# A fused adaLN, scan and SwiGLU kernel: the FFN's products in pairs of 64 rows instead of single products of 128

## The chip, the cores and the metric

The kernel runs on one core of a Trainium2 chip. Times are device microseconds of that core; the time of a kernel is the median of its runs. Lower is better.

## The reference

`x` is 2048 tokens (rows) by D = 448 channels, F = 1792, one state-space layer with N = 256 states a channel, all in float32.

```python
mod = (silu(c) @ w_mod).reshape(1, 6, 1, 448)         # sa, ca, ga, sb, cb, gb
h = layernorm(x) * (1 + ca) + sa
x = x + ga * S4(h)                                    # causal convolution over the 2048 rows + h * Dskip
h = layernorm(x) * (1 + cb) + sb
x = x + gb * ((silu(h @ w_gate) * (h @ w_up)) @ w_down)
```

Float32 accuracy is kept by splitting each operand of the large products into a high part in float32r and a remainder (`hi`, `lo`); three products are summed: hi times hi, hi times the weight's lo, lo times the weight's hi.

## The kernel before

The 2048 rows are 16 tiles of 128 rows. A preamble computes the modulation, the short form of the convolution (a cumulative sum over rows, a product with a triangular matrix `tri`, taken when a flag read at run time allows it; the profile is of that path) and the first two tiles. Then eight blocks of two tiles (256 rows) follow. In each, the FFN runs over NF = 14 chunks of 128 columns of F, called steps here, and the scan and the norms of the next block's two tiles are done beside it.

A step f, in the function `ffn`:

- `gate_up` (products at L758): h is kept transposed as `hhi`, `hlo`, four chunks of 128 channels by 256 rows. 448 channels are three and a half chunks; the last chunk holds the same 64 channels twice, once to meet the weight's hi, once its lo, so that hi times hi and hi times lo are seven products, lo times hi four: 11 for gate, then 11 for up, each of 256 columns into one bank of PSUM (`bank`, a pool of four).
- the gating: SILU on ACT (L773), its product with up on DVE (L788), `phi` on ACT (L795), `plo` on DVE (L796). The last step of a block does this in two halves (L781 to L784).
- `down` (L808) of the step before: per tile three products of 448 columns, summed over the 14 steps in the banks `dn` (DN[0] and DN[1]). It stands behind the gate/up of step f, so `down(f - 1)` is asked for a whole step after its inputs' gate/up has ended. After the last step the sums are scaled by `gb` and added to x (L865, L866), and x is stored.
- in block 0 the weights come from memory and are split into hi and lo (`split_w` at L122 to L125, two steps ahead, and `split_d` at L115 to L117); later blocks find them split.

The scan's stages of a tile are `s0` (norm, two operations on DVE), `s1` (two products), `rows` and `s2` (add the carried row `run`, split into vh and vl), `s3`, `s4` (three products with `tri`, L978 to L980, into the bank CV and a pool bank) and `s5` (carry row, sums added to x). Then `n2.stat`, `n2.root` (POOL), `make_xn` (DVE, the root applied by ACT) and `turn` (a transpose by DVE and five transfers through memory). `split_turned` writes the next block's `hhi` and `hlo`, with the shift `sbc` added.

Nothing schedules this at run time: the order of a queue is the order in which the program is written. `TIMES` gives for each stage the half step (two to a step) behind which it is written: `todo[(f, 0)]` ahead of the down products, `todo[(f, 1)]` behind.

## Time and profile before

| | |
|---|---|
| time, median of 3 runs (range) | 466.75 us (466.59 to 467.31) |
| span of the profiled execution | 465.0 us |
| lying around the span, taken against the median | 1.7 us |
| PE busy | 455.2 us, 98% |
| weight loads (PEld) busy | 434.4 us, 93% |
| DVE busy | 294.4 us, 63% |
| ACT busy | 171.7 us, 37% |
| first gate/up product of block 0 | 32.6 us into the span |

The profile is of one execution. PE is the matmul itself, PEld its weight load, which runs beside the matmul before. In a timeline row the first number is the start, the second how long the row's group lasted; a trailing bracket is the engine's idle time before it and what ended it. [...]

### The profile page before, as it was taken

To read this page: it belongs to the slowest core of one execution; us is meant where nothing else is said; L and a number is where in the kernel's file an instruction comes from. 1 tells how busy PE (TensorE), PEld (TensorE's weight loads), DVE (VectorE), ACT (ScalarE), POOL (GpSimd) and SP (SyncE) were. 2 spreads that over 40 slices of the span, in tenths; PEclk is the share of its full clock that TensorE was granted. 3 is DMA by queue.
4 is the path that set the end of the run, shared out by engine and by line. 5 is a ranking of instruction groups with operands and counts; after the bars stand their busy time and mean duration, and the time that the engine had idled before them with its cause. 6 is when DMAs were issued, how large, how long until landed. Compare 5 with 4: busy or idle time off the path is not lost.

```text
span 465.0 us, 8496 instructions
## 1 busy us (share of the span) xinstructions
PE 455.2 (98%) x3339; PEld 434.4 (93%) x3339; DVE 294.4 (63%) x614; ACT 171.7 (37%) x433; POOL 74.3 (16%) x99
## 2 busy tenths in 40 slices
PE   7899999999999999999999999999999999999996
PEld 4469999999999999999999999999999999999995
DVE  4888999868736676457746766467745775353224
ACT  4889656522333233322323233322333223332121
POOL 2142001000110521023210431005210331000000
PEclk9999999999999999999999999999999999999999
DMA  8975553010112001120022001120012101110001
GB/s 301 406 266 176 196 196 107 24 57 2 47 45 81 1 0 48 47 79 2 28 65 80 1 0 47 47 80 0 24 56 58 37 2 45 47 61 23 1 1 45
DMA packets 20947, 32.92 MB, mean 71 GB/s; under 512 B 2849, under 2 KB 15265, under 8 KB 20897
## 3 DMA queue, kind: packets, MB, share of 16 engines
q1 hardware_dynamic: 20256, 32.10, 20.0%
q8 instruction: 28, 0.46, 0.4%
q10 hardware_dynamic: 640, 0.18, 0.2%
q14 instruction: 23, 0.18, 0.1%
HBM read 25.40 MB, written 6.82 MB: 69 GB/s over the span
## 4 chain that ended last, share of the span: by engine, by line
PE 95%; issue 2%; DMA 1%; DVE 1%; POOL 0%; ACT 0%; POOLq 0%; ACTq 0%
PE bank L758 61%; PE dn L808 28%; DMA vec<-in_c_log_dt_dram 1%; PE dn L480 1%; PE cv L978 1%; PE bank L979 1%; PE cv L980 1%; PE bank L266 0%; PE bank L403 0%; POOL rsa L186 0%; PE cv L991 0%; PE bank L437 0%; ACT L339 0%; PE bank L836 0%; PE cv L375 0%
## 5 line engine op out<-in xcount | busy, mean ns | idle before, releaser
L758 PE MATMUL bank<-hhi,gu 128*128 128x256 f32 x1568 | 216.4, 278 | 0.1
L758 PEld LDWEIGHTS bank<-hhi,gu 128*128 128x128 f32 x1568 | 203.7, 188 | 3.7 <-issue 0.8
L758 PE MATMUL bank<-hlo,gu 128*128 128x256 f32 x896 | 138.6, 277 | 0.0
L758 PEld LDWEIGHTS bank<-hlo,gu 128*128 128x128 f32 x896 | 118.5, 188 | 0.2
L788 DVE TENSOR_TENSOR bank<-raw,bank 128x256 f32<-128x256 f32 x91 | 38.7, 426 | 82.1 <-PE bank L758 69.3
L795 ACT CAST phi<-bank 128x256 fp32r<-128x256 f32 x104 | 38.7, 372 | 132.4 <-DVE bank L788 132.4
L773 ACT ACTIVATE raw<-bank 128x256 f32<-128x256 f32 x98 | 37.5, 383 | 90.5 <-PE bank L758 86.9
L796 DVE TENSOR_TENSOR plo<-bank,phi 128x256 fp32r<-128x256 f32 x104 | 44.1, 424 | 40.8 <-ACT phi L795 40.8
L808 PE MATMUL dn<-wdh,phi 128*128 128x448 f32 x220 | 62.3, 364 | 0.0
L808 PE MATMUL dn<-wdh,plo 128*128 128x448 f32 x220 | 62.2, 363 | 0.0
L808 PE MATMUL dn<-wdl,phi 128*128 128x448 f32 x220 | 61.7, 362 | 0.0
L808 PEld LDWEIGHTS dn<-wdh,plo 128*128 128x128 f32 x220 | 41.2, 188 | 2.9 <-DVE plo L796 0.3
L808 PEld LDWEIGHTS dn<-wdl,phi 128*128 128x128 f32 x220 | 41.2, 187 | 2.6
L808 PEld LDWEIGHTS dn<-wdh,phi 128*128 128x128 f32 x220 | 34.8, 188 | 0.8 <-ACT p L773 0.2
L185 POOL TENSOR_SCALAR rsb<-mvb 128x1 f32<-128x1 f32 (+1 forms) x15 | 8.8, 584 | 115.0 <-DVE mvb L157 115.0
L185 POOL TENSOR_SCALAR rsa<-mva 128x2 f32<-128x2 f32 x8 | 1.9, 243 | 134.2 <-DVE mva L157 131.9
L215 ACT ACTIVATE raw<-raw,rsb 128x64 f32<-128x64 f32 x14 | 4.9, 349 | 34.6 <-POOL rsb L186 33.6
L125 DVE TENSOR_TENSOR gu<-raw,gu 128x1024 fp32r<-128x1024 f32 x14 | 17.1, 1219 | 0.9 <-ACT gu L123 0.9
L953 POOL TENSOR_TENSOR m<-m,gm 128x448 f32<-128x448 f32 x10 | 11.5, 1154 | 25.2 <-DVE m L202 25.2
L959 DVE TENSOR_TENSOR v<-v,run 1x448 fp32r<-1x448 f32 x14 | 13.3, 949 | 0.0
L967 DVE TENSOR_TENSOR vl<-m,vh 128x448 fp32r<-128x448 f32 x12 | 7.4, 617 | 8.9 <-ACT vh L966 8.8
L972 POOL TENSOR_TENSOR m<-m,gd 128x448 f32<-128x448 f32 x10 | 12.9, 1292 | 0.4
(240 smaller groups left out, 425.5 us busy)
## 6 DMA issues: line engine op xcount, KB each, us to landing
raw<-in_B_w_gate_up_dram SPq DMA_DIRECT2D x14, 512.0 KB, 3.3
rawd<-in_B_w_down_dram SPq DMA_DIRECT2D x16, 224.0 KB, 3.5
xd<-raw SPq DMA_DIRECT2D x12, 256.0 KB, 2.0
raw<-xd SPq DMA_DIRECT2D x48, 64.0 KB, 1.9
x<-in_A_u_dram SPq DMA_DIRECT2D x12, 224.0 KB, 2.9
out_dram<-x SPq DMA_DIRECT2D x11, 224.0 KB, 2.0
wm<-in_w_mod_groups_dram SPq DMA_DIRECT2D x5, 448.0 KB, 8.3
wm<-in_w_mod_groups_dram SPq DMA_DIRECT2D x5, 336.0 KB, 8.2
```

Of the source, the lines that this page charges most:

```text
L125: ve.tensor_tensor(wgu[j][:, :, 3:7, :], w[:, :, ::-1, :], f32(wgu[j][:, :, 0:4, :][:, :, ::-1, :]), op=OP.subtract)
L185: po.tensor_scalar(rs[:, 0:n], self.mv[:, 0:n, 1], EPS, None, op0=OP.add)
L758: pe.matmul(ps[s][:, 0:n], w[:, s, a], (hlo if lo else hhi)[:, k, first_col(n):first_col(n) + n], start=first and q == 0, stop=end and q = ...
L773: sc.activation(p[:, 0:n], ps[0][:, 0:n], AF.Silu)
L788: ve.tensor_tensor(ps[1][:, 0:n], p[:, 0:n], ps[1][:, 0:n], op=OP.mult)
L795: sc.copy(hi[:, 0:n], ps[1][:, 0:n])
L796: ve.tensor_tensor(lo[:, 0:n], ps[1][:, 0:n], f32(hi[:, 0:n]), op=OP.subtract)
L808: pe.matmul(dn[q][:, 0:D], u[:, cs], v, start=f == 0 and z == 0, stop=f == (NF - 3 if last else NF - 1) and z == 2)
L953: (ve if on_v else po).tensor_tensor(v, h, g, op=OP.mult)
L959: ve.tensor_tensor(v1[0:1], f32(v1[0:1]), run1[0:1], op=OP.add)
L967: ve.tensor_tensor(vl, v0, f32(vh), op=OP.subtract)
L972: (ve if on_v else po).tensor_tensor(h, h, gd, op=OP.mult)
```

## The change

The transposed h and the gate and up weights are laid out in seven chunks of 64 channels. Partitions 0 to 63 of a weight chunk hold gate, 64 to 127 hold up; h stands twice, in both halves. A product uses 64 rows of the array, and products are issued in pairs, one on the upper and one on the lower 64 rows (`both`): gate above into one bank, up below into another, 21 pairs a step (7 chunks times three parts). The weight load of a step is 448 KB instead of 512 KB.

The down sums are pairs too. Of a chunk of 128 columns of F the upper half holds 64, the lower half the other 64. In step f (`point`) the upper rows work for one tile and the lower rows for the other (`first`, of step f - 1); what is left, the other halves, follows at the next step's point (`rest`, of step f - 2), with the halves' tiles exchanged. So at a point each bank is written by one half alone. A point stands behind `POINT[f]` gate/up pairs: 18, and 14 in a block's first and last step. A block's last sums therefore fall into steps 0 and 1 of the next block, and there `leave` scales and stores them; blocks take the banks DN[0], DN[1] and DN[2], CV in turn (`SUMS`). The scan's three products with `tri` become six halves over two points, in the other block's banks.

Besides: the norm's root and shift are applied on DVE in `make_xn`; `split_turned` has no shift to add, and writes 1792 columns of hlo where 1024 were; `ident` lives in the preamble alone, block 0 turns its next tiles through memory as the others do; `TIMES` has ten entries a tile.

```diff
+POINT = [14] + [18] * 12 + [14]
-    ((2, 3), 3, ((4, 5, 7, 8, 10, 11, 12), (7, 8, 13, 14, 16, 17, 18))),
+    ((2, 3), 3, ((4, 5, 7, 8, 10, 12, 13, 13, 14, 16), (7, 8, 14, 15, 16, 18, 18, 18, 19, 20))),
...
+    SUMS = [DN[0:2], [DN[2], CV]]
...
     def make_xn(i, to):
...
+        ve.scalar_tensor_tensor(to, xs[i], m, cbw, op0=OP.subtract, op1=OP.mult)
+        ve.scalar_tensor_tensor(to, to, rs, sb, op0=OP.mult, op1=OP.add)
...
+    def split_turned(part):
+        for ks in (LOW, HIGH):
+            for q in range(2):
+                src = turned[q].rearrange("p a k r -> p k a r")[:, ks]
+                hi, lo = (h[:, ks, cols(q)].rearrange("p k (a r) -> p k a r", a=4) for h in (hhi, hlo))
+                if part == 0:
+                    sc.copy(hi, src)
+                else:
+                    ve.tensor_tensor(lo, src, f32(hi), op=OP.subtract)
...
+        def both(top, low):
+            done = []
+            for pair in zip_longest(top, low):
+                for e, op in zip(halves, pair):
+                    if op:
+                        o, w, r, start, stop = op
+                        done.append(pe.matmul(o, w[e], r[e], start=start, stop=stop).ins)
+            return done
...
+            def gate_up(f):
+                w, ps = wgu[f], [bank(), bank()]
+                prod = [(0, hhi), (1, hhi), (0, hlo)]
+                if fresh and f < 2:
+                    order = [(z, k) for z in range(3) for k in range(7)]
                 else:
+                    order = [(z, k) for k in range(7) for z in range(2)] + [(2, k) for k in range(7)]
+                ops = [(w[:, prod[z][0], k], prod[z][1][:, k], q == 0, q == 20) for q, (z, k) in enumerate(order)]
+                return ps, [[(t[:, 0:n], *o) for t in ps] for o in ops]
...
+            def first(f):
+                def half(c, begin, end):
+                    return [[(*down(f, q, z), begin and z == 0, end and z == 2) for z in range(3)] for q in (c, 1 - c)]
+                rest.append((half(1 - f % 2, False, f == (NF - 3 if last else NF - 1)), leave if f == NF - 1 else None))
+                return half(f % 2, f == 0, False)
+            def leave():
+                for q, i in enumerate(ts):
+                    ve.tensor_tensor(sums[q][:, 0:D], sums[q][:, 0:D], gb, op=OP.mult)
+                    ve.tensor_tensor(xs[i], xs[i], sums[q][:, 0:D], op=OP.add)
+                    sy.dma_start(out[i * 128:(i + 1) * 128, :], xs[i])
...
+            def point(f):
+                take = first if f else ahead.pop() if ahead else None
+                left = [rest.pop()] if rest else []
+                ops = [[], []]
+                if take and not (last and f == NF - 1):
+                    ops = take((f - 1) % NF)
+                for g, i in todo.get((f, "pe"), []) + todo.get((f - 1, "pe2"), []):
+                    ops = [u + v for u, v in zip(ops, g(i))]
...
+                for more, _ in left:
+                    ops = [u + v for u, v in zip(ops, more)]
+                done = both(*ops)
...
             for f in range(NF):
...
+                ps, ops = gate_up(f)
+                ops = list(zip(*ops))
+                both(ops[0][:POINT[f]], ops[1][:POINT[f]])
+                point(f)
+                both(ops[0][POINT[f]:], ops[1][POINT[f]:])
+                if f == NF - 1 and not last:
+                    split_turned(0)
+                gating(f, ps, f + 2 if fresh and f + 2 < NF else None)
+                if f == NF - 1 and not last:
+                    split_turned(1)
...
+        def first_half(i):
+            h, vh, vl, v1 = vs[i]
+            o, r = sums_for(i)
+            return [(o, tri, vh, True, False), (o, tri, vl, False, False)], [(r, tri, v1, True, False)]
+        def second_half(i):
+            h, vh, vl, v1 = vs[i]
+            o, r = sums_for(i)
+            return [(r, tri, v1, False, True)], [(o, tri, vh, False, False), (o, tri, vl, False, True)]
```

In the new kernel every product of the FFN has one line (L753, in `both`), the gating keeps L788, L795 and L796, SILU is L774, `leave` is L818 and L819, `make_xn` L209 and L210, the split weights L124 and L126, the hlo of the next block L255.

PE, one step of a steady block, before: 22 gate/up products (gate's 11, then up's 11), then the six down products of the step before.

```order
L758 MATMUL bank<-hhi,gu_609 128x256 x7
L758 MATMUL bank<-hlo,gu_609 128x256 x4
L758 MATMUL bank<-hhi,gu_609 128x256 x7
L758 MATMUL bank<-hlo,gu_609 128x256 x4
L808 MATMUL dn_68<-wdh_664,phi 128x448
L808 MATMUL dn_69<-wdh_664,phi 128x448
L808 MATMUL dn_68<-wdl_665,phi 128x448
L808 MATMUL dn_69<-wdl_665,phi 128x448
L808 MATMUL dn_68<-wdh_664,plo 128x448
L808 MATMUL dn_69<-wdh_664,plo 128x448
```

PE, a step after: 36 halves (18 pairs), then at the point the newest step's three pairs and, of the step before that, the other halves (four of their six products are shown; six more gate/up halves follow).

```order
L753 MATMUL bank<-hhi,gu_984 128x256 x28
L753 MATMUL bank<-hlo,gu_984 128x256 x8
L753 MATMUL dn_68<-wdh_1062,phi 128x448
L753 MATMUL dn_69<-wdh_1062,phi 128x448
L753 MATMUL dn_68<-wdl_1063,phi 128x448
L753 MATMUL dn_69<-wdl_1063,phi 128x448
L753 MATMUL dn_68<-wdh_1062,plo 128x448
L753 MATMUL dn_69<-wdh_1062,plo 128x448
L753 MATMUL dn_68<-wdh_986,phi 128x448
L753 MATMUL dn_69<-wdh_986,phi 128x448
L753 MATMUL dn_68<-wdl_987,phi 128x448
L753 MATMUL dn_69<-wdl_987,phi 128x448
```

The down products of the newest step moved from behind the next step's 22 gate/up products to behind 18 of its 21 pairs, and half of each step's sums moved one step later.

DVE, the boundary of two steady blocks, before: the last step's gating in halves, the next block's hlo, the four operations that scale the sums and add them to x, then the gating of step 0.

```order
L781 TENSOR_TENSOR raw<-raw,bank 128x128 x2
L784 TENSOR_TENSOR plo<-raw,phi 128x128 x2
L220 SCALAR_TENSOR_TENSOR hlo<-raw,sbc,hhi 128x256 x4
L865 TENSOR_TENSOR dn_68<-dn_68,gb 128x448
L866 TENSOR_TENSOR x_74<-x_74,dn_68 128x448
L865 TENSOR_TENSOR dn_69<-dn_69,gb 128x448
L866 TENSOR_TENSOR x_75<-x_75,dn_69 128x448
L788 TENSOR_TENSOR bank<-raw,bank 128x256
```

DVE, the same place after:

```order
L781 TENSOR_TENSOR raw<-raw,bank 128x128 x2
L784 TENSOR_TENSOR plo<-raw,phi 128x128 x2
L255 TENSOR_TENSOR hlo<-raw,hhi 128x4x128 x2
L255 TENSOR_TENSOR hlo<-raw,hhi 128x3x128 x2
L788 TENSOR_TENSOR bank<-raw,bank 128x256
L796 TENSOR_TENSOR plo<-bank,phi 128x256
L818 TENSOR_TENSOR dn_70<-dn_70,gb 128x448
L819 TENSOR_TENSOR x_74<-x_74,dn_70 128x448
L818 TENSOR_TENSOR cv<-cv,gb 128x448
L819 TENSOR_TENSOR x_75<-x_75,cv 128x448
L788 TENSOR_TENSOR bank<-raw,bank 128x256
```

The four operations moved behind the gating of step 0 and stand ahead of that of step 1; they read sums that PE ends in step 1.

DVE, a steady block, steps 8 to 10 before: `s5` of the second tile (L1000 to L1003), a gating, its statistics and the one operation of `make_xn` (L212), the next gating.

```order
L981 TENSOR_TENSOR x_73<-m_79,x_73 128x448
L1000 SCALAR_TENSOR_TENSOR run<-run,cv 32x448
L1002 TENSOR_TENSOR x_73<-x_73,cv 128x448
L1003 SCALAR_TENSOR_TENSOR x_73<-bank,tok,x_73 128x448
L788 TENSOR_TENSOR bank<-raw,bank 128x256
L796 TENSOR_TENSOR plo<-bank,phi 128x256
L156 BN_STATS stb<-x_73 128x6
L157 BN_AGGR mvb<-stb 128x2
L212 SCALAR_TENSOR_TENSOR raw<-x_73,mvb,cbw 128x448
L788 TENSOR_TENSOR bank<-raw,bank 128x256
```

DVE, the same work after, between the gatings of steps 9 and 10:

```order
L796 TENSOR_TENSOR plo<-bank,phi 128x256
L1032 SCALAR_TENSOR_TENSOR run<-run,dn_70 32x448
L1034 TENSOR_TENSOR x_73<-x_73,dn_70 128x448
L1035 SCALAR_TENSOR_TENSOR x_73<-cv,tok,x_73 128x448
L157 BN_STATS stb<-x_73 128x6
L158 BN_AGGR mvb<-stb 128x2
L209 SCALAR_TENSOR_TENSOR raw<-x_73,mvb,cbw 128x448
L210 SCALAR_TENSOR_TENSOR raw<-raw,rsb,sb 128x448
L788 TENSOR_TENSOR bank<-raw,bank 128x256
```

All seven operations now stand in one gap between two gatings, and L210 reads `rsb`, the root that POOL computes from L158's result.

## The prediction

> **What bounds the kernel now.** I read the page's busy times, then the chain that ended last, then the timeline of one step.

> ```profile
> span 465.0 us, 8496 instructions
> PE 455.2 (98%) x3339; PEld 434.4 (93%) x3339; DVE 294.4 (63%) x614; ACT 171.7 (37%) x433; POOL 74.3 (16%) x99
> PE bank L758 61%; PE dn L808 28%; DMA vec<-in_c_log_dt_dram 1%; PE dn L480 1%; PE cv L978 1%; PE bank L979 1%; PE cv L980 1%; PE bank L266 0%; PE bank L403 0%; POOL rsa L186 0%; PE cv L991 0%; PE bank L437 0%; ACT L339 0%; PE bank L836 0%; PE cv L375 0%
> ```

> PE is busy almost throughout, and its gate/up products (L758) and down products (L808) are 89% of the chain. A step f of the FFN, in order of time:

> ```profile
> 203.17 0.96 PE L758 MATMUL bank<-hhi,gu 128*128 128x256 f32 x7
> 204.42 0.56 PE L808 MATMUL dn<-wdh,phi 128*128 128x448 f32 x2
> 206.88 0.96 PE L758 MATMUL bank<-hhi,gu 128*128 128x256 f32 x7
> ```

> The 11 products of the up half run from 203.17 to 204.42, 0.1136 us each. One step is 206.88 - 203.17 = 3.71 us: 22 such products (2.50) and six of 448 columns (1.21, 0.2017 each). So a column costs 0.44 to 0.45 ns in both, and the stream has no gap. There are 8 x 14 = 112 steps. The span lies 1.7 us under the median of the runs (466.75); I sum against 465.0 and add that back.

> **The change: the products.** Gate/up goes from 22 products to 21 pairs, down from 6 to 6 pairs. What a pair of 64-row products costs, no row shows. Ends: 0.1136, since each half still streams its 256 columns, so I exclude less; and 0.227, two in turn. The nearest rows are the preamble's products in column tiles, beside whole-array products of the same length (25.34 to 26.09: two passes, 0.375 each):

> ```profile
> 17.20 0.57 PE L266 MATMUL bank<-wm,cs 128*32 128x448 f32 x3
> 17.60 0.55 PE L266 MATMUL bank<-wm,cs 128*32 128x448 f32 x3
> 25.34 0.92 PE L480 MATMUL dn<-v,tri 128*128 128x448 f32 x2
> 26.09 0.92 PE L480 MATMUL dn<-hd,ident 128*128 128x448 f32 x2
> 17.20 0.12 PEld L266 LDWEIGHTS bank<-wm,cs 128*32 128x32 f32 x3 [0.17 <-issue]
> L266 PEld LDWEIGHTS bank<-wm,cs 128*32 128x32 f32 x24 | 0.7, 107 | 0.7 <-issue 0.4 <-DMA wm<-in_w_mod_groups_dram 0.2
> L758 PEld LDWEIGHTS bank<-hhi,gu 128*128 128x128 f32 x1568 | 203.7, 188 | 3.7 <-issue 0.8
> ```

> Three tiles' passes take 0.40 us, what one alone takes, and three loads of 107 ns are over in 0.12. Tiles of the array work side by side, so I take 0.1136 and 0.2017 a pair: **-0.1136 x 112 = -12.7 us**, and a step of 21 x 0.1136 + 6 x 0.2017 = 3.60.

> A load grows by (188 - 107)/96 = 0.84 ns a column, so 128 columns hold the load path 108 of every 114 ns. [...]

> Scan products: three of 448 columns a tile before, now six halves in two points, where each point has eight on one half and seven on the other: four pair times instead of three, 14 tiles x 0.20 = **+2.8**. The end of block 0 loses its PE transposes and two tiles their two-pass products: **-1** (estimate from their few 0.1 us each).

> **The change: what PE now waits for.** Before, gate ended half a step before up, so SILU (L773) lay beside up. Now gate and up end together. Let T be the time at which a step's last gate/up product has been streamed. The rows of the chain, once with SILU as the last to come, once with SILU after its products (the next products start at 241.49):

> ```profile
> 236.38 0.36 ACT L773 ACTIVATE raw<-bank 128x256 f32<-128x256 f32 x1
> 236.77 0.43 DVE L788 TENSOR_TENSOR bank<-raw,bank 128x256 f32<-128x256 f32 x1 [2.12 <-ACT raw L773]
> 237.24 0.37 ACT L795 CAST phi<-bank 128x256 fp32r<-128x256 f32 x1 [0.50 <-DVE bank L788]
> 237.64 0.42 DVE L796 TENSOR_TENSOR plo<-bank,phi 128x256 fp32r<-128x256 f32 x1 [0.44 <-ACT phi L795]
> 241.49 0.96 PE L758 MATMUL bank<-hhi,gu 128*128 128x256 f32 x7
> 241.75 0.38 ACT L773 ACTIVATE raw<-bank 128x256 f32<-128x256 f32 x1 [1.61 <-PE bank L758]
> 82.39 0.42 DVE L796 TENSOR_TENSOR plo<-bank,phi 128x256 fp32r<-128x256 f32 x1
> 82.86 0.30 PEld L808 LDWEIGHTS dn<-wdh,plo 128*128 128x128 f32 x2 [0.28 <-DVE plo L796]
> ```

> SILU starts 0.26 after T, the product L788 at T+0.65, phi ends at T+1.49, plo at T+1.94; PE takes it 0.05 later. The new order asks for phi after 18 pairs (T+2.05) and for plo two down pairs on (T+2.45). Cushion: 2.45 - 1.99 = 0.46 us. Before, the down products came a whole step after T, and a late L788 did no harm:

> ```profile
> 223.58 0.56 PE L808 MATMUL dn<-wdh,phi 128*128 128x448 f32 x2
> 225.97 0.42 DVE L788 TENSOR_TENSOR bank<-raw,bank 128x256 f32<-128x256 f32 x1
> 227.90 0.56 PE L808 MATMUL dn<-wdh,phi 128*128 128x448 f32 x2
> ```

> Here L788 ran 2.39 after T, and PE did not wait. Now DVE is free at T+1.94 and the next L788 is due at T+3.60+0.65 = T+4.25: 2.30 us of other DVE work fit, 0.46 more goes into the cushion, and beyond 2.76 PE waits. By the new order, a block of the steady kind:

> ```profile
> 196.49 0.62 DVE L865 TENSOR_TENSOR dn<-dn,gb 128x448 f32<-128x448 f32 x1
> 198.89 0.42 DVE L788 TENSOR_TENSOR bank<-raw,bank 128x256 f32<-128x256 f32 x1
> 193.58 0.48 DVE L781 TENSOR_TENSOR raw<-raw,bank 128x128 f32<-128x128 f32 x2 [2.43 <-PE bank L758]
> 103.41 0.60 DVE L958 TENSOR_TENSOR m<-m,run 1x448 f32<-1x448 f32 x1
> 105.19 0.68 DVE L200 SCALAR_TENSOR_TENSOR m<-rawd,mva,ca 128x448 f32<-128x448 f32 x1
> 106.51 0.42 DVE L788 TENSOR_TENSOR bank<-raw,bank 128x256 f32<-128x256 f32 x1
> 65.25 0.63 DVE L1000 SCALAR_TENSOR_TENSOR run<-run,cv 32x448 f32<-32x448 f32 x1
> 67.16 0.61 DVE L117 TENSOR_TENSOR wdl<-rawd,wdh 128x448 fp32r<-128x448 f32 x1
> 233.10 0.62 DVE L156 BATCH_NORM_STATS2 stb<-x 128x6 f32<-128x448 f32 x1
> 233.75 0.18 DVE L157 BATCH_NORM_AGGREGATE mvb<-stb 128x2 f32<-128x6 f32 x1
> 234.82 0.57 POOL L186 TENSOR_TENSOR rsb<-rsb,halves 128x1 f32<-128x1 f32 x1
> 53.23 0.83 ACT L122 CAST gu<-raw 128x768 fp32r<-128x768 f32 x1
> 59.09 1.22 DVE L125 TENSOR_TENSOR gu<-raw,gu 128x1024 fp32r<-128x1024 f32 x1
> 60.22 0.42 DVE L796 TENSOR_TENSOR plo<-bank,phi 128x256 fp32r<-128x256 f32 x1
> ```

> - **leave** (four operations, 196.49 to 198.89, 2.40 us) now stands between the sums of step 1 and its L788. Those sums end three pairs (0.34) before T; add 0.26 for the lag: DVE is through at T+2.32, L788 is 1.67 late, PE waits 1.67 - 0.46 = 1.21.
> - **hlo of the next block**: from L781 (193.58) to the end of the old hlo work (196.49) are 2.91; it had 1024 columns in four, now 1792, at L125's rate (1.13/1024) 0.38 longer. So the low four chunks are there at about T+3.2 and the rest at T+4.07; PE asks at T+2.80, and four pairs later. Waits 0.42 and 0.40.
> - **Steps 4 and 8**: rows, vl, and two s0 operations take 3.10 (103.41 to 106.51): 0.34 over. At step 8 the same amount follows a step 7 that ends 0.46 late; less 0.40 for the longer point: 0.40.
> - **Step 10**: s5 (65.25 to 67.16, 1.91), statistics (0.65), then make_xn, which now needs the root on DVE (before, ACT applied it): 1.64 from the aggregate's start to the root's end, and 0.66 for its second operation (half of 105.19 to 106.51). 1.94 + 1.91 + 0.65 + 1.64 + 0.66 = T+6.80 against T+4.25: wait 2.10.

> Seven boundaries x 2.03 = **+14.2**; six blocks x 2.84 = **+17.0**. In block 0 each step also splits weights ahead of plo: cast from T+0.54 to T+1.51 (0.83 x 896/768), L126 for 0.99, plo at T+2.94, usable 0.54 too late; eleven times 5.9, some 2 more where the scan's work crowds: **+8**. Queues of POOL and SP get no work that PE waits for; a turn has as many transfers as before and nothing behind it but the split at step 13. Preamble: one more DVE operation (0.66) and an ACT copy stand ahead of the first gate/up; SILU lies bare at the end: **+1.2** (0 to 1.6).

> Sum: -12.7 + 2.8 - 1 + 14.2 + 17.0 + 8 + 1.2 = **+29.5**, a span of 494.5, a time of **496 us**. All waits could be zero, or, with no cushion, about 0.46 x 45 places = 20 more.

> **Rivals.**
> - *The waits don't reach PE*, and the change is faster. What speaks for it: DVE is only 63% busy, and a 2.39 us delay cost nothing before. Against: that had a step to spare. Price: 465.0 - 9.7 + 1.7 = 457 us. It decides where the waits of leave, of step 10 and of block 0 sum to less than 9.7 us, a quarter of my 39.2.
> - *The halves' loads come in turn*: 2 x 108 = 216 ns for every pair, 27 x 0.216 = 5.83 a step, +2.12 x 112 = +238, about 704 us (steps so long hide the waits). For it: the load path is already held 108 of 114 ns. Against: the three loads in 0.12 us.
> - *Pairs are slowed a little*, by twice as many instructions: 20 ns a pair would be 27 x 0.02 x 112 = 60 us, less the waits that fit in the longer steps, some 20: 536. No row decides it.

> **How the numbers follow.** Forecast as summed, 478 to 520: 0.54. Waits hidden, 453 to 463: 0.24. Waits of about 10 us that just eat the gain: 0.04. Pairs slowed, 520 to 640: 0.10. Loads in turn: 0.08. The range 453 to 540 leaves out the last, half of the one before and the ends. Faster 0.24, same 0.04 (within 0.2%, about what a measurement tells), slower 0.72.

> **What would show it.** Right: 42 gate/up products in about 2.4 us where nothing is late; PE idle in front of phi, plo and hlo products, released by DVE and ACT, about 2 us in step 11 and 1.2 in step 2 of each block, half a microsecond in most steps of block 0. Wrong: no idle time of PE there, or pairs well over 0.114 us.

## The result and the profile after

The changed kernel takes 550.41 us (median of 4 runs, 549.06 to 552.33), the kernel before 466.72 beside it: a ratio of 1.180, 95% interval 1.177 to 1.182. The forecast was slower, with 496 us and a range up to 540; 550 lies above that range, and the kernel is slower by nearly three times the 29.5 us that the sum gave. The profiled execution has a span of 550.3.

The page of the kernel after: span, busy times, granted clock in 40 slices (9 is full speed) and the chain that ended last.

```profile
span 550.3 us, 14319 instructions
PE 483.5 (88%) x6271; PEld 442.9 (80%) x6271; DVE 314.7 (57%) x625; ACT 159.4 (29%) x390; POOL 72.5 (13%) x103
PEclk9999999899999988899889998899988999999999
PE 46%; DVE 23%; ACT 8%; issue 5%; DMA 2%; POOL 1%; SPq 1%; DVEq 0%; ACTq 0%
```

Before, 89% of the chain were PE's products; now PE has 46% and VectorE 23%. And the clock row has eights in it, at regular distances. The kernel before had nines alone:

```profile
PEclk9999999999999999999999999999999999999999
```

The pairs themselves do what the prediction took. An undisturbed step (PE's timeline; x28 counts both halves, so 14 pairs):

```profile
247.44 1.75 PE L753 MATMUL bank<-hhi,gu 64*128 64x256 f32 x28
249.02 0.62 PE L753 MATMUL bank<-hlo,gu 64*128 64x256 f32 x8
249.47 0.36 PE L753 MATMUL cv<-wdh,phi 64*128 64x448 f32 x1
249.48 0.36 PE L753 MATMUL dn<-wdh,phi 64*128 64x448 f32 x1
249.67 0.36 PE L753 MATMUL cv<-wdl,phi 64*128 64x448 f32 x1
251.03 1.75 PE L753 MATMUL bank<-hhi,gu 64*128 64x256 f32 x28
```

251.03 - 247.44 = 3.59 us a step, against 3.71 before and 3.60 forecast. In this step the two halves' products start within 0.01 us of one another, 14 pairs take 249.02 - 247.44 = 1.58, 0.113 each, and a pair of 448 columns 0.20. (These are distances between starts; a single product of 256 columns is recorded as lasting 0.27 us.)

What PE waited for, over the whole span (us, times, longest), the longest groups in the blocks:

```profile
PE dn L753 <- ACT phi L795: 23.0, 19, 2.3
PE dn L753 <- ACT vh L999: 16.9, 7, 2.9
PE cv L753 <- ACT phi L795: 3.6, 4, 0.9
PE bank L753 <- ACT hhi L253: 2.9, 1, 2.9
PE dn L753 <- DVE plo L796: 2.9, 9, 0.7
```

One steady block holds these waits (step 2, step 5, step 8, step 11 and the boundary), and is 64.7 us long against 53.1 before (windows of the two kernels from a block's first down product to the next block's; after the times come the busy times of PE, PEld, DVE, ACT and POOL, the granted clock, the DMA share and GB/s):

```profile
242.10 0.47 PE L753 MATMUL cv<-wdh,phi 64*128 64x448 f32 x1 [0.91 <-ACT phi L795]
254.23 0.47 PE L753 MATMUL dn<-wdh,phi 64*128 64x448 f32 x1 [1.00 <-ACT phi L795]
269.69 0.47 PE L753 MATMUL dn<-vh,tri 64*128 64x448 f32 x1 [2.83 <-ACT vh L999]
284.99 0.68 PE L753 MATMUL dn<-wdh,phi 64*128 64x448 f32 x1 [1.96 <-ACT phi L795]
285.48 0.57 PE L753 MATMUL dn<-wdl,phi 64*128 64x448 f32 x1
299.64 0.62 PE L753 MATMUL bank<-hlo,gu 64*128 64x256 f32 x6 [0.20 <-DVE hlo L255]
237.41:302.14 64.73, 57.59 (x772) 54.33 (x770) 35.65 (x70) 14.79 (x37) 10.04 (x12) 0.95 0.12 37
```
```profile
200.71:253.84 53.13, 53.13 (x400) 52.02 (x399) 32.93 (x68) 16.17 (x41) 10.72 (x12) 1.00 0.12 38
```

The wait for vh is not in the prediction. VectorE and ScalarE ahead of it, step 7 of that block:

```profile
266.25 1.43 DVE L209 SCALAR_TENSOR_TENSOR raw<-x,mvb,cbw 128x448 f32<-128x448 f32 x1
267.78 0.68 DVE L210 SCALAR_TENSOR_TENSOR raw<-raw,rsb,sb 128x448 f32<-128x448 f32 x1
268.38 0.61 DVE L991 TENSOR_TENSOR m<-m,run 1x448 f32<-1x448 f32 x1
269.07 0.56 ACT L999 CAST vh<-m 128x448 fp32r<-128x448 f32 x1 [3.20 <-DVE m L991]
```

make_xn for the first tile (L209, L210) stands ahead of the row addition of the second (L991), vh is cast behind that, and the scan's first product is asked in step 8's point, 18 pairs after the step's start.

And behind the two longest waits of this block (2.83 and 1.96 us) the granted clock is 0.50. Windows of the same block:

```profile
244.00:250.00 6.00, 6.00 (x96) 5.90 (x96) 3.58 (x7) 1.52 (x4) 3.54 (x5) 1.00 0.01 3
271.50:275.00 3.50, 3.50 (x38) 3.50 (x37) 1.91 (x4) 0.76 (x2) 0.00 (x0) 0.52 0.00 0
275.00:278.00 3.00, 3.00 (x44) 2.99 (x43) 0.27 (x1) 0.38 (x1) 0.00 (x0) 1.00 0.41 127
285.00:288.00 3.00, 3.00 (x20) 2.76 (x22) 0.95 (x2) 0.00 (x0) 0.00 (x0) 0.51 0.21 76
```

From 271.43 to 274.84 and from 285.08 to 288.50 the granted clock is 0.50, and PE counts as busy: this loss is in no list of waits. The block's mean is 0.95, so it loses 0.05 x 64.7 = 3.2 us; over the span it is (1 - 0.961) x 550.3 = 21 us, of which 1 stands behind PE's last product. The blocks differ: the one before this has a clock of 0.92 (5.2 us), and in block 1 no half clock follows the waits of 2.03 (vh) and 1.98 us (step 11).

A steady block in sum, by the distances between steps: 14 steps of 3.59 and 1.6 for the scan's pairs are 51.9, and 12.8 come on top: labelled waits 7.1, half clock 3.2, and some 2.5 of restarts behind each wait and hlo waits too short for a label (an estimate, by difference).

### The profile page after: what moved, and what is told of

Read it like the earlier page. It is cut to its first block, busy times and chain, and to the rows that moved or that the text cites. A ratio compares the mean times of both kernels' runs of the same rounds, so it can differ in the third digit from the quotient of the medians.

```text
span 550.3 us, 14319 instructions
## 1 busy us (share of the span) xinstructions
PE 483.5 (88%) x6271; PEld 442.9 (80%) x6271; DVE 314.7 (57%) x625; ACT 159.4 (29%) x390; POOL 72.5 (13%) x103
## 4 chain that ended last, share of the span: by engine, by line
PE 46%; DVE 23%; ACT 8%; issue 5%; DMA 2%; POOL 1%; SPq 1%; DVEq 0%; ACTq 0%
PE bank L753 26%; PE dn L753 16%; PE cv L753 4%; DVE bank L788 3%; ACT phi L795 3%; DMA raw<-xd 2%; DVE hlo L255 2%; ACT raw L774 2%; DVE raw L209 2%; DVE stb L157 1%; DVE run L1032 1%; DVE m L991 1%; DVE x L1035 1%; DVE v L992 1%; DVE dn L818 1%
## 5 line engine op out<-in xcount | busy, mean ns | idle before, releaser
L753 PE MATMUL bank<-hhi,gu 64*128 64x256 f32 x3136 | 214.6, 284 | 3.3 <-ACT hhi L253 2.9
L753 PEld LDWEIGHTS bank<-hhi,gu 64*128 64x128 f32 x3136 | 204.1, 193 | 4.1 <-ACT hhi L253 3.1
L753 PE MATMUL bank<-hlo,gu 64*128 64x256 f32 x1568 | 140.4, 283 | 1.5 <-DVE hlo L255 1.2
L753 PEld LDWEIGHTS bank<-hlo,gu 64*128 64x128 f32 x1568 | 128.0, 191 | 7.3 <-DVE hlo L255 5.0
L753 PE MATMUL dn<-wdh,phi 64*128 64x448 f32 x332 | 92.1, 392 | 23.1 <-ACT phi L795 23.0
L788 DVE TENSOR_TENSOR bank<-raw,bank 128x256 f32<-128x256 f32 x91 | 38.8, 426 | 122.2 <-ACT raw L774 120.2
L774 ACT ACTIVATE raw<-bank 128x256 f32<-128x256 f32 x98 | 37.7, 385 | 221.5 <-PE bank L753 221.5
L753 PE MATMUL dn<-wdh,plo 64*128 64x448 f32 x332 | 88.9, 385 | 3.0 <-DVE plo L796 2.9
L753 PE MATMUL dn<-wdl,phi 64*128 64x448 f32 x332 | 87.2, 371 | 0.0
L753 PEld LDWEIGHTS dn<-wdh,phi 64*128 64x128 f32 x332 | 46.3, 190 | 28.3 <-ACT phi L795 27.0
L796 DVE TENSOR_TENSOR plo<-bank,phi 128x256 fp32r<-128x256 f32 x104 | 44.1, 424 | 40.4 <-ACT phi L795 40.4
L795 ACT CAST phi<-bank 128x256 fp32r<-128x256 f32 x104 | 38.8, 373 | 87.8 <-DVE bank L788 87.8
L753 PEld LDWEIGHTS dn<-wdh,plo 64*128 64x128 f32 x332 | 46.3, 191 | 12.1 <-DVE plo L796 10.4
L753 PEld LDWEIGHTS dn<-wdl,phi 64*128 64x128 f32 x332 | 47.0, 191 | 1.2
L753 PE MATMUL cv<-wdh,phi 64*128 64x448 f32 x108 | 41.3, 382 | 3.6 <-ACT phi L795 3.6
L753 PE MATMUL cv<-wdh,plo 64*128 64x448 f32 x108 | 40.5, 375 | 0.0
L753 PE MATMUL cv<-wdl,phi 64*128 64x448 f32 x108 | 39.8, 368 | 0.0
L186 POOL TENSOR_SCALAR rsb<-mvb 128x1 f32<-128x1 f32 x16 | 6.7, 420 | 172.3 <-DVE mvb L158 171.7
L753 PE MATMUL dn<-vh,tri 64*128 64x448 f32 x28 | 11.4, 406 | 16.9 <-ACT vh L999 16.9
L753 PEld LDWEIGHTS cv<-wdh,phi 64*128 64x128 f32 x108 | 20.3, 188 | 4.5 <-ACT phi L795 4.4
L186 POOL TENSOR_SCALAR rsa<-mva 128x2 f32<-128x2 f32 x8 | 1.8, 231 | 158.0 <-DVE mva L158 155.5
L753 PEld LDWEIGHTS cv<-wdh,plo 64*128 64x128 f32 x108 | 20.4, 189 | 1.6 <-DVE plo L796 1.1
```

Of the source, the lines that this page charges most:

```text
L186: po.tensor_scalar(rs[:, 0:n], self.mv[:, 0:n, 1], EPS, None, op0=OP.add)
L753: done.append(pe.matmul(o, w[e], r[e], start=start, stop=stop).ins)
L774: sc.activation(p, ps[0][:, 0:n], AF.Silu)
L788: ve.tensor_tensor(ps[1][:, 0:n], p, ps[1][:, 0:n], op=OP.mult)
L795: made[f] = sc.copy(hi, ps[1][:, 0:n]).ins.name
L796: ve.tensor_tensor(lo, ps[1][:, 0:n], f32(hi), op=OP.subtract)
```

## The experiments

My theory (A) after that: the pairs are worth what was forecast; the new order asks too early for phi, plo, vh and hlo; and PE's idle time of a couple of microseconds lowers the clock, which costs again as much as a wait. The main rivals: the pairs themselves lower the clock (B), or cost something else that undisturbed steps don't show (D).

**make_xn behind vh.** Times of make_xn and turn for the first tile, blocks 1 to 6:

```diff
-    ((2, 3), 3, ((4, 5, 7, 8, 10, 12, 13, 13, 14, 16), ...
+    ((2, 3), 3, ((4, 5, 7, 8, 10, 12, 13, 13, 16, 17), ...
```

> In blocks 1 to 6 the two VectorE operations of make_xn for the first tile move from ahead of the second tile's vh (step 7) to step 8; nothing else changes. Theory A (PE's idle time is what lowers the granted clock): the wait for vh in step 8 falls from 2.84 to about 0.7 us, and the half-speed stretch behind it (about 2.6 us a block) goes with it; part comes back, since step 8 now carries 1.4 us more of VectorE work: 6 x (2.1 + 2.6 - 0.7) = 24, about 526 us, mean granted clock from 0.961 to about 0.98. Theory B (the lower clock comes from the pairs themselves, not from the idle time): only the wait goes, 6 x 2.1 = 13, about 538 us at a clock of 0.96.

Measured: 536.34 us (532.98 to 538.74), ratio 1.148 (1.144 to 1.152). A block:

```profile
266.11 0.47 PE L753 MATMUL dn<-vh,tri 64*128 64x448 f32 x1 [1.48 <-ACT vh L999]
281.26 0.47 PE L753 MATMUL dn<-wdh,phi 64*128 64x448 f32 x1 [1.97 <-ACT phi L795]
281.57 0.36 PE L753 MATMUL dn<-wdl,phi 64*128 64x448 f32 x1
236.68:298.53 61.85, 56.08 (x772) 52.15 (x770) 35.73 (x71) 14.78 (x37) 10.02 (x12) 0.97 0.13 39
```

The wait for vh halves rather than falling to 0.7 (the row additions now run beside POOL), 1.35 us a block, and the block gains 2.9. So about as much comes from the clock as from the wait, which B doesn't give; but A's 526 was too much, and 536 is nearer to B's 538, so this run alone doesn't settle it. The second row shows a wait as long as that of the kernel after (1.97, 1.96) that is not followed by half speed: the next product stands 0.31 us behind, against 0.49 there.

**Useless products in place of idle time.**

```diff
+PAD = {8: 12, 11: 8}
...
+                if not fresh and not last:
+                    both(*([(*t[0][:3], True, True)] * PAD.get(f, 0) for t in ops))
                 both(ops[0][:POINT[f]], ops[1][:POINT[f]])
```

> Useless work: in blocks 1 to 6 the first gate/up pair of step 8 is multiplied 12 times more and that of step 11 eight times more, 12 x 0.1136 = 1.36 and 8 x 0.1136 = 0.91 us of PE time. The operands that PE waits for come from VectorE and ScalarE at the same time as before, so the waits shrink to about 1.5 (vh) and 1.05 us (phi). Theory A (idle time over some 1 to 2 us halves the clock for the next 3 to 4 us): the half-speed stretches go, 6 x 4.8 = 29 us less, about 521 us, clock near 0.99: more work and less time. Theory B (pairs lower the clock by themselves): no change, 550 us or a little more, clock 0.96 or less.

Measured: 539.62 us (538.89 to 542.98), ratio 1.159 (1.155 to 1.164). The same stretch of a block, the vh wait, and a step of the last block:

```profile
265.34 0.46 PE L754 MATMUL dn<-vh,tri 64*128 64x448 f32 x1 [1.54 <-ACT vh L1002]
279.10 0.47 PE L754 MATMUL dn<-wdh,phi 64*128 64x448 f32 x1 [1.05 <-ACT phi L796]
233.00:294.70 61.70, 56.99 (x810) 53.63 (x810) 35.58 (x70) 14.85 (x37) 10.05 (x12) 1.00 0.13 39
502.78 1.81 PE L754 MATMUL bank<-hhi,gu 64*128 64x256 f32 x28
```

With 2.3 us more work in it, the block is 3.0 us shorter, and its clock is 1.00. B is out: the same pairs run at full clock once PE has no long pause (in five of the blocks 1 to 6; in the sixth the clock halved once more, behind a vh wait of 1.54). The size was wrong again: I had counted 4.8 us of half clock a block, and 3.2 are there to be won; and of the 18 us that six such blocks would give, the span shows 12. Many undisturbed steps of this run take 3.69 in place of 3.59 us (1.81 against 1.75 in the row of 14 hhi pairs), at a granted clock of 1.00; the kernel after has such steps too (260.17 to 263.86). What decides between 3.59 and 3.69 I don't know; no run was made for it.

**leave behind the gating.**

```diff
-                    if then:
-                        then()
+                    if then:
+                        late.append(then)
...
                 gating(f, ps, f + 2 if fresh and f + 2 < NF else None)
+                if late:
+                    late.pop()()
```

> The four operations of leave (2.40 us of VectorE) are written behind step 1's gating in place of ahead of it. Theory A (what counts is how much VectorE has to do between two gatings, 2.3 us and the cushion of 0.46): the wait of 0.91 us in step 2 goes, but step 1 now carries leave and the statistics, 4.0 us, 1.7 over the room, so a wait of about 1.2 us appears in step 3: 550 us, within 3. Theory C (only what stands between the sums and the product with SILU counts): the wait goes and none comes, 7 x 1.27 = 9 us less, 541.

Measured: 553.59 us (552.8 to 555.79), ratio 1.189 (1.186 to 1.192). Step 2 is now free and step 3 waits:

```profile
245.49 0.47 PE L753 MATMUL dn<-wdh,phi 64*128 64x448 f32 x1 [0.83 <-ACT phi L795]
```

As A has it: what counts is VectorE's work between two gatings, not on which side of a gating it stands. Step 3 is 1.17 us longer than an undisturbed one, 1.2 were expected; the time lies 0.6 us above the 550 within 3. C, 541 us, falls.

**The kernel before, made to wait.** Whole-array products, no pairs; useless copies ahead of phi.

```diff
+                for _ in range(SLOW.get((b, f), 0)):
+                    sc.copy(p[:, 0:n], p[:, 0:n])
                 sc.copy(hi[:, 0:n], ps[1][:, 0:n])
```

> The kernel before, whole-array products and no pairs, with 7 to 14 useless ScalarE copies of 0.38 us ahead of phi in steps 3 and 11 of blocks 1 to 6, so that PE waits for phi there between about 0.4 and 3.1 us, each length once or twice. Theory A: behind the long waits (from about 2 us) the products run at half speed for some 3 to 4 us, 0.227 in place of 0.1136 us for 256 columns, and behind those of 1 us and less they don't; the span grows by the sum of the waits (about 20) and by some 1.5 to 2 us for each of the about six long ones: 465 + 20 + 10 = 495. Theory B: products keep 0.1136 us behind every wait, 485.

Measured: 497.75 us (one run), span 496.0. Four of its waits, and the granted clock behind them:

```profile
141.07 1.11 PE L812 MATMUL dn<-wdh,phi 128*128 128x448 f32 x2 [3.66 <-ACT phi L799]
201.00 0.67 PE L812 MATMUL dn<-wdh,phi 128*128 128x448 f32 x2 [2.41 <-ACT phi L799]
259.89 0.68 PE L812 MATMUL dn<-wdh,phi 128*128 128x448 f32 x2 [1.97 <-ACT phi L799]
342.03 0.67 PE L812 MATMUL dn<-wdh,phi 128*128 128x448 f32 x2 [2.41 <-ACT phi L799]
141.00:144.40 3.40, 3.33 (x11) 3.08 (x12) 1.18 (x3) 0.67 (x3) 0.00 (x0) 0.50 0.00 0
144.40:146.80 2.40, 2.40 (x13) 2.40 (x13) 0.00 (x0) 0.38 (x1) 0.00 (x0) 0.50 0.00 0
201.60:205.00 3.40, 3.40 (x15) 3.22 (x14) 0.56 (x2) 0.37 (x1) 0.00 (x0) 0.50 0.00 0
260.00:263.40 3.40, 3.40 (x26) 3.31 (x27) 1.05 (x3) 0.88 (x3) 0.00 (x0) 1.00 0.02 5
342.00:345.40 3.40, 3.37 (x24) 3.28 (x25) 3.25 (x6) 0.85 (x2) 0.00 (x0) 1.00 0.00 0
```

So the clock halves behind idle time in this kernel too, without a pair in it. Waits of 0.2 to 1.97 us (nine of them) cost 0.3 us beyond themselves, by the distances between steps; 2.84 and 3.66 cost 1.8 and 3.0 beyond themselves; of two waits of 2.41 one cost 1.9 and the other 0.4. The span is 31.0 us longer: 21.7 of waits, some 6 of half clock and 3 of restarts.

In the kernel after, the record of the granted clock holds twelve stretches of 0.50: ten of 3.41 us, one of 6.83 (203.16 to 209.99), and one from 547.91 on, behind the last product. All twelve start whole multiples of 3.413 us apart (203.16, 220.23, 271.43, 285.08 and 336.28: 5, 15, 4 and 15 multiples). The windows of this run agree with that length: 0.50 from 201.6 to 205.0 and 1.00 from 205.5, 0.50 from 141.0 to 146.8 and 1.00 from 147.5. Waits of 1.96 us (the kernel after) and 2.41 (this run) were followed by such a stretch, and in the next run a labelled wait of 1.23.

Laid on this grid of 3.413 us, pauses that were followed by half clock stand apart from some of the same length that were not. In this run the grid is an estimate, laid on its stretch from 201.62. Of the two waits of 2.41, the one from 198.59 to 201.00 lies whole in the window that ends at 201.62, where the clock halves; the one from 339.63 to 342.03 is divided by an edge at 341.56 into 1.94 and 0.47, and from 342.0 on the clock is 1.00. In block 1 of the kernel after, edges at 141.7 and 155.4 divide the waits of 2.03 and 1.98 in the same way: no window there has more than 1.29 us of idle time, and the clock stays at 1.00.

**The sums one step later.** The largest edit: phi and plo have three buffers, a point takes up the sums of the steps two and three back, and waits for the SILU of the step before alone (that wait orders the two halves' writes to one bank). The product with SILU goes to SBUF, scan products come last in a point, make_xn behind vh as above.

```diff
-                take = first if f else ahead.pop() if ahead else None
+                take = first if f > 1 else ahead.pop() if ahead else None
...
-                    ops = take((f - 1) % NF)
+                    ops = take((f - 2) % NF)
...
-                ve.tensor_tensor(ps[1][:, 0:n], p, ps[1][:, 0:n], op=OP.mult)
+                u = ps[1][:, 0:n] if fresh else p
+                ve.tensor_tensor(u, p, ps[1][:, 0:n], op=OP.mult)
...
-            ahead[:] = [first]
+            ahead[:] = [first, first]
```

> The pairs are kept, and the sums of a step are asked one step later (phi and plo of step f in steps f+2 and f+3, three buffers of each, the product with SILU kept in SBUF so that the banks come free earlier, scan products last in their point, make_xn for the first tile behind vh). A point waits only for the SILU of the step before. Theory A (the pairs are worth their 12.7 us, and what made the kernel slower is asked too early): PE's waits for phi and plo in the blocks go (26 and 3 us), vh waits fall under 1 us, no half-speed stretches, clock 0.99 or more; steps of 3.60; what stays is hlo (0.8 a block) and about 10 us of block 0 and the boundary behind it: 458 to 468 us. Theory D (the pairs cost something that the undisturbed steps don't show, such as the exchange of the banks between the halves): 480 us or more without waits in the trace.

Measured: 514.24 us (512.25 to 515.92), ratio 1.102 (1.098 to 1.106). What PE waits for now:

```profile
PE bank L755 <- ACT hhi L255: 11.4, 7, 4.7
PE dn L755 <- ACT vh L1004: 9.6, 7, 2.2
219.57:277.29 57.72, 53.77 (x772) 51.59 (x770) 37.01 (x70) 15.05 (x37) 10.45 (x12) 1.00 0.14 42
```

phi has gone from the list (26.6 us before, in two groups), and a steady block falls from 64.7 to 57.7, this one at full clock. In two of the six, half speed follows vh's wait of 1.23; whether the scan's half-filled pairs around it had a part in that, no run shows:

```profile
310.00:313.30 3.30, 3.30 (x38) 3.30 (x37) 1.93 (x5) 0.79 (x2) 0.00 (x0) 0.55 0.00 0
```

Neither forecast held: hhi, which was on time in the steady blocks, is late now that PE comes to the boundary sooner, and vh is still late.

**Those waits one by one.** gd x h of the scan on VectorE, half of each turn's transfers from ScalarE's queue, hlo ahead of the last gating, the table of times for block 0. In this kernel make_xn of block 0 takes over the buffer of one weight block before that is split, so it doesn't compute the reference and is read for its times only; the run after it has this mended.

```diff
                     split_turned(0)
+                    split_turned(1)
                 gating(f, ps, f + 2 if fresh and f + 2 < NF else None)
-                if f == NF - 1 and not last:
-                    split_turned(1)
...
+            (sy if z < 2 else sc).dma_start(...)
```

> The delayed sums as in the run before, and the waits that its trace still shows taken up one by one: gd x h of the scan goes to VectorE (POOL's operation beside them made the row additions 1.56 us in place of 0.61), the second half of the turn's transfers is issued from ScalarE's queue, hhi and hlo are cast tile by tile and hlo ahead of the last gating, the casts of the gated weights come two steps behind their product, block 0 follows the table of the other blocks. Theory A (all that the pairs lost is waits and the half clock behind them): vh (1.23 a block), hhi and boundary (about 2.4 a block) mostly go, a steady block falls from 57.8 to about 52, block 0 gives some 8: 514 - 6 x 5.5 - 8 - 3 = 470, within 8; against 466.7 of the kernel before, so that the pairs' own gain of 12.7 would be eaten up to where block 0 and the head stand. Theory D (the pairs cost something else): it stays above 490 with few waits left.

Measured: 481.36 us (479.32 to 483.01), 3 us above the 470 within 8. A steady block is 54.4, 1.3 above the 53.1 of the kernel before, with hhi's wait still in it, so theory D has little room left.

Next, the sums of step 8 two pairs later and x loaded a block earlier (the edit in part):

```diff
-POINT = [14] + [18] * 12 + [14]
+POINT = [14] + [18] * 7 + [20] + [18] * 4 + [14]
...
+                if b and b + 2 < len(TILES):
+                    for i in TILES[b + 2]:
+                        at(4, 0, load_x, i)
```

> As the run before, with four changes: in block 0 make_xn for the first tile one step later (behind the split of the weights whose buffer it takes over); a block's x tiles are loaded a block earlier, so that their transfers no longer run beside the turn's; block 0's fetches all on SP's queue; the sums of step 8 two pairs later, so that vh is there. Theory A: hhi (about 1.2 us a block) and vh (0.3 and its refill) go, a steady block falls from 54.2 to about 52.5, below the 53.1 of the kernel before; with block 0 some 10 us over: 481.4 - 6 x 1.7 - 2 = 469, within 5. If the pairs had a cost of their own beside the waits (theory D), the steady block would stay above 53.5 without a wait in it.

Measured: 481.44 us (479.39 to 484.98), ratio 1.032 (1.029 to 1.035): no gain over the run before, where 469 within 5 was expected. The steady block stays at 54.2. vh's label went away in the blocks, hhi's wait (6.5 us in six places) did not: the transfers of x beside the turn weren't the cause. VectorE, without a gap over 0.9 us from step 7 to step 10, turns the second tile too late. That suggested starting the chain sooner (the table of times alone is shown):

```diff
-    ((2, 3), 3, ((4, 5, 7, 8, 10, 12, 13, 13, 16, 17), (7, 12, 14, 15, 16, 18, 18, 18, 19, 20))),
+    ((0, 1), 1, ((2, 3, 5, 4, 8, 10, 13, 13, 14, 15), (6, 10, 12, 11, 14, 16, 17, 17, 18, 19))),
```

> As the run before, and from block 2 on the scan of the next block starts a step or two earlier (statistics in step 0, the two tiles' products at steps 4 and 7), so that the turned tiles are back before hhi is asked; gd x h on POOL again, but ahead of the row additions; block 0's carried rows go by ScalarE's queue and its scan operations on VectorE. Theory A: hhi's wait (1.1 a block) and step 8's lateness (0.75) go from block 2 on, a steady block is 52.2 (14 x 3.60 and 1.6 for the scan's pairs) against 53.1 of the kernel before, block 0 gains about 3: 481.4 - 5 x 1.8 - 3 = 469, within 4. Theory E (VectorE's order is the bound of these blocks whatever their table: its 36 us of work have too few gaps): waits only move, 478 to 484.

Measured: 472.98 us (472.21 to 473.37), ratio 1.014 (1.012 to 1.016), within A's 469 within 4; E's 478 to 484 falls for these blocks. From block 2 on PE has no labelled wait. A steady block, and the two longest groups of waits that are left:

```profile
208.86:260.89 52.03, 51.91 (x773) 51.44 (x771) 34.38 (x70) 15.12 (x37) 9.39 (x13) 1.00 0.15 46
PE bank L758 <- ACT hhi L258: 3.2, 2, 2.1
PE dn L758 <- ACT vh L1013: 2.0, 1, 2.0
```

A steady block is 52.0 us, 1.1 below the 53.1 of the kernel before: D falls, and the pairs' gain is there nearly in full where nothing is late ((12.7 - 2.8)/8 = 1.2 a block). The waits that are left stand in block 0 and at the boundaries behind blocks 0 and 1.

**Block 0.** The second tile's rows and vh half a step sooner, every point at 20 pairs, both queues for block 0's fetches:

```diff
-    ((1, 3), 5, (..., (9, 12, 14, 15, 16, 18, 18, 19, 20, 21))),
+    ((1, 3), 5, (..., (9, 12, 13, 15, 16, 18, 18, 19, 20, 21))),
-POINT = [14] + [18] * 6 + [20] * 2 + [18] * 4 + [14]
+POINT = [14] + [20] * 12 + [14]
```

> As the run before, with three changes for block 0, where what is left over (about 9 us beside its products) stands: the row additions and vh of the second tile half a step earlier, the sums of every step two pairs later (0.23 us), the second half of each fetch on ScalarE's queue there too. Theory A: vh's wait of 2.0 us falls to about 0.4 and the half-clock stretch behind it (2 us) goes, the SILU waits (0.6, 0.7) fall by 0.2 each, hhi by 0.7: 473.0 - 5 = 468, within 2, still 1 to 3 us above the kernel before. Theory E (VectorE is full in block 0, with 20 us of scan work beside 33 of splits and gating): the wait only moves to plo or hhi, 471 to 474.

Measured: 475.82 us (474.53 to 477.25), ratio 1.019 (1.018 to 1.021). As E has it, and a little worse: vh's wait went, a wait of 2.70 for SILU came (ScalarE stands behind vh), and hhi's grew from 2.1 to 3.2. No version that I ran beats the kernel before; the nearest is 1.4% above it.

## Why the prediction was wrong, and where it was right

The forecast had the direction and the price of the pairs right. What failed is its sum of waits: the term for step 8 left out vh, that for step 4 was too small, block 0 was put at half of what it cost, and the clock was no term.

- **The products: right.** 3.59 us a step against 3.60, in some steps 3.69. So both rivals on the pairs' price fall: loads in turn (216 ns a pair) and pairs slowed by 20 ns (a step of 3.69 is 3 to 4 ns a pair more). The forecast had its price from products in column tiles of 32; for two row tiles no row of the kernel before showed it. In the step from 247.44 their products start within 0.01 us of one another. The halves' loads run side by side as well: they too start within 0.01 us of one another, and a pair takes 0.113 us with its loads. That a load of 64 rows takes as long as one of 128, as the 216 ns has it, no run had shown; the records have 184 ns (247.4 to 251.0) against 188 before. The scan's pairs: points with them make a step of 4.00, 0.4 more; four such points a block are 1.6 against 1.2 before, +2.8 over 14 tiles, as forecast.
- **The chain, leave, hlo and step 10 (whose wait stands in step 11): right.** leave was to cost 1.21 and costs 1.27 (a step of 4.86; 0.91 of it labelled). hlo: 0.82 forecast, a boundary step of 4.47 to 4.49, 0.9 over. Step 11: 2.10 forecast, 1.96 measured.
- **Step 4: mis-sized.** 0.34 forecast, 1.00 measured. I took the row additions from a row in which POOL did nothing. Here POOL works beside them:

```profile
249.68 1.42 POOL L1005 TENSOR_TENSOR m<-m,gd 128x448 f32<-128x448 f32 x1
250.00 1.58 DVE L992 TENSOR_TENSOR v<-v,run 1x448 fp32r<-1x448 f32 x1
```

- **Step 8: the wrong product.** I asked when L788 of that step would run, and got 0.40. The wait that ends last there is vh's, 2.83 and 0.19: the term left out the scan's own operands, for which the moved order asks as well. VectorE's work was taken too small there too: from L209 to the end of L1000 it is 4.05 us (266.25 to 270.30; L209 takes 1.43 beside POOL and 0.69 at 282.06), where 3.10 were taken, so that the term's own working would have given about 1.35 (an estimate). It is the prediction's bullet on steps 4 and 8 that failed.
- **The clock: not a term at all.** The sum took every product at full speed. Of blocks 1 to 6, half clock followed the wait for vh in five and the one in step 11 in four, mostly for 3.4 us each. That costs 3.2 us in the block shown and some 20 in all, block 0 with it.
- **Block 0: mis-sized.** +8 for its waits; from its first down product to the next block's it went from 55.8 to 72.6, +16.8. The half microseconds were there (0.2 to 0.9 in most steps), but step 8's phi (2.32, ScalarE held by statistics) and hhi (2.9, behind the turn's transfers) were not in the sum, nor the half clock behind each of them (some 3 us together).

From +29.5 to +85.3, by estimate: 20 for the clock, 14 for vh, 5 for step 4, some 6 in block 0 beside its half clock, and the rest restarts behind the waits. The rival with hidden waits (457 us) falls: the five groups of labelled waits above sum to 49.3 us.

## What to carry to other kernels

When an order is tightened, list everything the moved instructions read, not only the operand on which the change is centred, and ask of each when it comes: the scan's vh cost more than any of the waits that were foreseen. A change that gains 0.1 us a step and asks for its operands 1.7 us sooner (T+2.05 in place of T+3.71, T being the end of a step's gate/up) needs a consumer delayed by as much (here the sums one step later) before it can pay. And count a pause of PE of about 2 us nearly twice, once for itself and once for the half clock that followed it in some cases here (3.41 us at 0.50, about 1.7 us lost); pauses of 1 us cost little beyond themselves (0.3 us each in the kernel before, made to wait).
